# Head outputs copied once and stacked by on-chip transfers, and the low-part pass one unit later, in an adaLN block of attention and Mish feed-forward

## The chip, the cores and the metric

The kernel runs on one core of a Trainium2 chip. Its time is the device time of one execution in microseconds, the median of several. Matrix products run on TensorE (PE in the profile, its weight loads PEld), elementwise work on VectorE (DVE), ScalarE (ACT) and GpSimd (POOL); nearly all transfers are issued by SyncE (SP), one after the other, in the order of the program. An engine works through its own instructions in order; a semaphore wait at the head of a queue holds all that is behind it.

## The reference

One block with S = 2048 rows, D = 448, 16 heads of 28, a sliding window of 256 keys, a feed-forward width of 1792 and fp32 data:

```python
mod = (_silu(c) @ w_mod).reshape(c.shape[0], 6, 1, -1)
sa, ca, ga, sb, cb, gb = (mod[:, 0], mod[:, 1], mod[:, 2], mod[:, 3], mod[:, 4], mod[:, 5])
h = _layernorm(x, axis=-1) * (1 + ca) + sa
x = x + ga * _A_ref(h, A_wqkv, A_wo)     # windowed attention, softmax over (q-k >= 0) & (q-k < 256)
h = _layernorm(x, axis=-1) * (1 + cb) + sb
x = x + gb * _B_ref(h, B_w1, B_b1, B_w2) # dense, h * tanh(softplus(h)), dense
return x
```

## The kernel before

All products are made in fp32r with the operands split in two: a high part that ScalarE writes as fp32r and a low part, the difference. A product is then three passes (high x high, high x low, low x high).

**Groups, slots, units.** The 2048 rows are 4 groups of 512. In a group every head is a *slot* (64 in all, `NS`), and every slot has three *units* (192, `NU`) of 512 score columns: the blocks of keys that touch the window. The main loop (lines 1046 to 1107) runs over units `u`, with `s, k = divmod(u, 3)`: slot `s`, third `k`, group `g = s // 16`. What it issues in one step is the order of every engine's queue:

- `A(i, t)`: scores of slot `i`, 128 rows at a time, for the row maximum (TensorE into the bank `sA`, two buffers, then VectorE). It runs three slots ahead. `M2` turns the maxima of two slots into rows `mr`, and two small transfers put them into the extra rows of Q (`q<-mr`).
- `B(u)`: scores with keys on the partitions, masks added (bank `sB`, two buffers), then ScalarE's two exponentials from it: `P` in fp32 and `Ph` in fp32r, three buffers each.
- `SP(u-1)`: GpSimd's subtraction `Pl = P - Ph` (the last five units shared with VectorE).
- `PV`: products with V, high pass `PV(u-2, Ph)` at the end of a step, low pass `PV(u-3, Pl)` at the start of the next. V has 60 columns: 28 high, one of ones whose product is the softmax sum, and 28 low from column 32. So the bank `pv` of a head (two buffers) holds in rows 0 to 31 one part of its output and in rows 32 to 59 the other.
- `EV(i, part)`: ScalarE copies these two parts, one copy each, to the place of the head in `O4` and `OL4`, where four heads (a *quad*) stand one above the other at 32 partitions each. For the last three heads VectorE makes the second copy.
- For each quad `QA` (GpSimd, `O4 + OL4`), `T1` (VectorE, transposes in blocks of 32 and the reciprocal of the sums), `TM` (GpSimd, times the reciprocal), `T2` (VectorE, transposes back). After `T2` of the fourth quad of a group the group's attention is in `on_full`.
- `load_slot(s + 5)`: two transfers bring Q and K of a later slot from `scr` in HBM, where the projections are put. `need` first makes sure that the projection tiles of that head are stored: it flushes the stores that wait in `later` and, where a tile is missing, runs filler. The load waits on SyncE's queue for those stores to land.

**Filler.** Between these, `fill_main(g)` gives out the matmuls of other work as a generator: the rest of this group's projections (tiles 5, 2, 6), then, once `on_full` has the group before, its output projection (`gen_oT`, `gen_wo`), then the next group's transposed LayerNorm output (`gen_hT`) and its projections. Each piece tells its cost; each unit adds a credit `RATE[g]` (twice as much in the first units of a group, `FRONT`), and pieces are issued until the credit is spent. A step that waits for `on_full` costs one `RATE`. What is left at a group's end is issued in one go (`drain`). `fill_side` does the same for LayerNorm statistics and weights on the other engines, and `later` holds transfers that are issued one at a time.

**The end.** `TAIL` puts the first feed-forward matmuls between the last units; then the feed-forward stage (lines 1108 to 1181) follows.

In SBUF the pool `att` has the tiles `P`, `Ph` and `Pl` of 2 KB per partition and buffer. The transfers' scratch is left at its default size.

Of the kernel before, what the change touches and what calls it, by code (L numbers as in the profile page):

```python
# [8 lines left out]
F32 = mybir.dt.float32  # L9
F32R = mybir.dt.float32r  # L10
BF16 = mybir.dt.bfloat16
AF = mybir.ActivationFunctionType
ALU = mybir.AluOpType

S, D, F, H, DH, W = 2048, 448, 1792, 16, 28, 256
NG, GT = 4, 512
# [35 lines left out]
def adaln_block(ctx: ExitStack, tc: tile.TileContext, x, wqkv, wo, w1, b1, w2, c, w_mod, out):  # L52
    nc = tc.nc
    PE, ACT, DVE, POOL = nc.tensor, nc.scalar, nc.vector, nc.gpsimd
# [3 lines left out]
    def dma(o, i):  # L58
        nc.sync.dma_start(o, i)
# [31 lines left out]
    def bank(tag, bufs, name):  # L91
        return PS[0].tile([128, 512], F32, name=name, tag=tag, bufs=bufs)
# [163 lines left out]
    def tr_chunk(xs, ci, p):  # L256
        for t in range(4):
            PE.transpose(p[:, t * 128:(t + 1) * 128], xs[t][:, ci * 128:(ci + 1) * 128], ident)
# [5 lines left out]
    def hT_hi(p, ci, hh, si):  # L264
        ACT.activation(hh[:, ci], p, AF.Identity, scale=cols[:, si + 1, ci:ci + 1], bias=cols[:, si, ci:ci + 1])
# [6 lines left out]
    def new_T(key, pl):  # L272
        return (pl.tile([128, 4, GT], F32R, name=f"hh{key}", tag="hh"),
                pl.tile([128, 4, GT], F32R, name=f"hl{key}", tag="hl"))
# [20 lines left out]
    def gen_hT(g):  # L295
        drain(ln1[g])
        hh, hl = HT[g] = new_T(g, mid)
        for ci in range(4):
            p = bank("mm", 2, f"tr{g}{ci}")
            tr_chunk(XS[g], ci, p)  # L300
            pipe.add(2, lambda p=p, ci=ci: hT_hi(p, ci, hh, 0), lambda p=p, ci=ci: hT_lo(p, ci, hh, hl, 0))
            yield 1.9
        ht_done.add(g)
        if g + 1 < NG:
            loads = (lambda: x_load(g + 1),) if g > 1 else (lambda: (x_tile(g + 1), x_half(g + 1, 0)),
                                                            lambda: x_half(g + 1, 2))
            pipe.add(0, None, None, lambda: later.extend(loads))
# [5 lines left out]
    def drain(*gs):  # L313
        for g in gs:
            for _ in g:
                pipe.step()
# [17 lines left out]
    def flush():  # L334
        while later:
            later.pop(0)()
# [185 lines left out]
    att, att_s = pool("att")  # L522
# [1 line left out]
    Q3 = [Q2[i // 2][:, i % 2] for i in range(NQ)]  # L524
    k3_tile(att, NK - 1)

    O4, OL4, T4 = [att.tile([128, GT], F32, name=n) for n in ("o4", "ol4", "t4")]
    POOL.memset(OL4, 0.0)
    wo3 = [mid.tile([128, D], F32R, name=f"wo3_{i}", tag="wo", bufs=8) for i in range(4)]
    wol = [mid.tile([128, D], F32R, name=f"wol_{i}", tag="wo", bufs=8) for i in range(4)]  # L530
# [143 lines left out]
    NS = NG * H  # L674
    mx, Pt, Ph, Pl, pvb = {}, {}, {}, {}, {}
# [34 lines left out]
    def B(u):  # L710
        i, b = divmod(u, 3)
        g, h = divmod(i, H)
        q, k = Q3[i % NQ], K3[i % NK]
        bl = units(g, b)
        c0 = bl[0][3]
        p = bank("sB", 2, f"sB{u}")
        for n, (jj, t0, t1, c) in enumerate(by_width(bl)[::-1]):
            PE.matmul(p[:, c:c + 128 * (t1 - t0)], k[:, jj * 128:(jj + 1) * 128], q[:, t0 * 128:t1 * 128],  # L718
                      start=(n == 0), stop=False, skip_group_check=True)
        far = {c + 128 * (jj - t0) for jj, t0, t1, c in bl if t0 <= jj < t1}  # L720
        diag = {c + 128 * (jj - 2 - t0) for jj, t0, t1, c in bl if t0 <= jj - 2 < t1}
        masked = []
        for c in sorted(far | diag):
            if c in far:
                masked.append((256 if c + 128 in diag else 128, c, 0))
            elif c - 128 not in far:
                masked.append((128, c, 128))
        for n, c, m in sorted(masked):
            PE.matmul(p[:, c:c + n], identr, fdmask[:, m:m + n], start=False, stop=True, skip_group_check=True)  # L729
        P = Pt[u] = att.tile([128, 512], F32, name=f"P{u}", tag="P", bufs=3)  # L730
        Ph[u] = att.tile([128, 512], F32R, name=f"Ph{u}", tag="Ph", bufs=3)
        ACT.activation(P[:, c0:], p[:, c0:], AF.Exp, scale=SCALE)  # L732
        ACT.activation(Ph[u][:, c0:], p[:, c0:], AF.Exp, scale=SCALE)  # L733

    def SP(u):
        i, b = divmod(u, 3)
        c0 = units(i // H, b)[0][3]
        Pl[u] = att.tile([128, 512], F32R, name=f"Pl{u}", tag="Pl", bufs=3)
        for eng, a, b in ((POOL, c0, 512),) if u < NU - 5 else ((POOL, 0, 256), (DVE, 256, 512)):
            eng.tensor_tensor(Pl[u][:, a:b], Pt[u][:, a:b], Ph[u][:, a:b].bitcast(F32), op=ALU.subtract)  # L740

    def PV(u, P):
        i, b = divmod(u, 3)
        g, h = divmod(i, H)
        if P is Ph and b == 0:
            pvb[i] = bank("pv", 2, f"pv{i}")
        pv = pvb[i]
        for n, (jj, t0, t1, c) in enumerate(by_width(units(g, b))):
            j = 4 * g - 2 + jj
            PE.matmul(pv[0:60, t0 * 128:t1 * 128], V[j % NV][:, h, :], P[u][:, c:c + 128 * (t1 - t0)],  # L750
                      start=(P is Ph and b == 0 and n == 0), stop=False, skip_group_check=True)

    def EV(i, part):
        a = i % 4 * 32
        if part == 0:
            ACT.activation(O4[a:a + 32], pvb[i][0:32, :], AF.Copy)
        elif i < NS - 3:
            ACT.activation(OL4[a:a + DH], pvb[i][32:60, :], AF.Copy)
        else:
            DVE.tensor_copy(OL4[a:a + DH], pvb[i][32:60, :])  # L760

    def quad(qd):
        g, ci = divmod(qd, 4)
# [4 lines left out]
    def QA(qd):  # L768
        o, t = quad(qd)
        for eng, a, b in ((POOL, 0, GT),) if qd < NS // 4 - 1 else ((POOL, 0, 192), (DVE, 192, GT)):  # L770
            eng.tensor_tensor(o[:, a:b], O4[:, a:b], OL4[:, a:b], op=ALU.add)
# [3 lines left out]
    def T1(qd):  # L775
        o, t = quad(qd)
        DVE.transpose(T4, o)
        rcq[qd] = att.tile([128, 16, 1], F32, name=f"rc{qd}", tag="rc", bufs=1)
        DVE.reciprocal(rcq[qd], t[:, :, 28:29])
# [6 lines left out]
    def T2(qd):  # L786
        o, t = quad(qd)
        DVE.transpose(o, T4)
        if qd % 4 == 3:
            on_full.add(qd // 4)  # L790
# [204 lines left out]
        if not (told.get(g) == "bank" and pipe.held() or told.get(g) in taken):  # L995
            told[g] = next(side[g], None)

    RATE = {0: 0.64, 1: 1.02, 2: 1.02, 3: 0.65}
    FRONT = {0: 0, 1: 2, 2: 2, 3: 2}
    ln1 = {g: gen_ln1(g) for g in range(1, NG)}  # L1000
    fillers = {g: fill_main(g) for g in range(NG)}
# [2 lines left out]
    def step(g):  # L1004
        return next(fillers[g], 99.0) or RATE[g]

# [37 lines left out]
    NU = 3 * NS  # L1044
    credit = 0.0
    for u in range(NU + 9):
        s, k = divmod(u, 3)
        g = s // H
        if k == 0 and s % H == 0 and 0 < g < NG:
            drain(fillers[g - 1], side[g - 1])  # L1050
            flush()
        pipe.step()
        if 0 <= u - 3 < NU:
            PV(u - 3, Pl)
            if k == 2 and s % 4 != 1:
                EV(s - 1, 0)
        if k == 0 and 0 <= s - 2 < NS:
            if s % 4 == 2:
                EV(s - 2, 0)
            EV(s - 2, 1)  # L1060
        qd = (s - 5) // 4
        if k == 1 and s % 4 == 1 and 0 <= qd < NS // 4:
            QA(qd)
        if u < NU:
            B(u)
        if 0 <= u - 1 < NU:
            SP(u - 1)
        a = s + LEAD
        if a < NS:
            A(a, (0, 1, 3)[k])  # L1070
        if k == s % 2 and s < NS:
            load_slot(s + LEAD + 2)
        if k == 2 and s % 4 == 1 and 0 <= qd < NS // 4:
            T1(qd)
        qd = (s - 6) // 4
        if s % 4 == 2 and 0 <= qd < NS // 4:
            if k == 0:
                TM(qd)
            if k == (2 if u < NU else 0):
                T2(qd)  # L1080
        if g < NG:
            v = u - 48 * g
            if v in (0, 12):
                chunk["v"] = 4 if v == 0 and g or 0 < g < NG - 1 else 2
            if v == 0:
                credit = 0.0
            credit += RATE[g] * (2 if v < FRONT[g] else 1)
            while credit > 0.0:
                credit -= step(g)
        if k == 0 and (a - 1) % 2 == 1 and LEAD <= a - 1 < NS:  # L1090
            M2((a - 1) // 2)
        if g < NG:
            if v > 1 or g == 0:
                side_step(g, ("dve", "act")[a >= NS:] if k == 1 else ("act",) if k == 0 and s % 2 == 0 else ())
            if later and ((s + (k == 2)) % 2 == 0 or k == 1):
                later.pop(0)()
        if u == NU:
            drain(fillers[NG - 1], side[NG - 1])
            while pipe.items:
                pipe.step()  # L1100
            flush()
        if u - NU in TAIL:
            TAIL[u - NU]()
        if k == 1 and a < NS:
            A(a, 2)
        if 0 <= u - 2 < NU:
            PV(u - 2, Ph)
# [53 lines left out]
    for n in range(NN + 1):  # L1161
        g, f = divmod(n, NF)
# [44 lines left out]
```

## Time and profile before

| | |
|---|---|
| median of 3 runs | 729.16 us (728.52 to 729.28) |
| the profiled execution | 729.9 us |
| its span, first to last instruction | 728.1 us |
| mean granted clock of TensorE | 0.983 |
| bytes moved by transfers | 83.74 MB, 115 GB/s on the mean |

The main loop's first unit begins about 47 us after the start of the span, and the last attention output is copied at about 430 us. In rows of the profile a name such as `Pl<-P,Ph` is the tile written and those read; L740 is a line of the kernel; "x192 | 234.1, 1226 | 95.1" are the count, the busy time in us, the mean duration in ns, and the idle time of the engine before them in us. Rows of waits give the total in us, how often, and the longest. SPq stands for SyncE's queue, whose rows are issues of transfers and not their duration; `q<-mr` or `k<-scr` names a transfer as destination and source. A wait that depends on several semaphores is put down to the one that came last.

### The profile page before, as it was taken

The numbers are of one execution on the slowest core, as the hardware profiler recorded it, in microseconds if no ns is written. First come the engines' busy times: TensorE is split into PE (matmuls) and PEld (weight loads), VectorE is DVE, ScalarE is ACT, GpSimd is POOL, SyncE is SP. The second block draws the span as 40 slices with busy tenths as digits, with TensorE's granted clock in tenths as the row PEclk, the third lists the DMA queues.
The fourth block names the chain that finished last, engine by engine and source line by source line (L and its number), as shares of the span: only waits on it lengthen the run. The fifth ranks groups of instructions, "written<-read, shape, count | busy, mean of one in ns | idle before, by whom it ended". The sixth has DMA issues, their size and how long they took to land.

```text
span 728.1 us, 11809 instructions
## 1 busy us (share of the span) xinstructions
PE 688.9 (95%) x3873; PEld 582.3 (80%) x3873; DVE 399.7 (55%) x992; ACT 429.5 (59%) x784; POOL 348.7 (48%) x363
## 2 busy tenths in 40 slices
PE   8998989989989989999999889999999999999996
PEld 7776767779778778788778668888888888888885
DVE  5678657668847668765788876242424133323112
ACT  4559878788857688877898984334233223322221
POOL 6536778687846687856888947332010000000002
PEclk9999999989999989999999999999999999999998
DMA  7854763364373354275484145500200020001001
GB/s 221 256 197 165 213 187 127 107 204 147 83 251 120 102 184 159 72 232 152 147 274 154 53 137 181 151 14 1 101 1 1 0 102 1 0 1 51 0 1 50
DMA packets 48330, 83.74 MB, mean 115 GB/s; under 512 B 6287, under 2 KB 26429, under 8 KB 48269
## 3 DMA queue, kind: packets, MB, share of 16 engines
q1 hardware_dynamic: 47804, 82.98, 36.4%
q8 instruction: 31, 0.51, 0.3%
q14 instruction: 31, 0.25, 0.1%
q10 hardware_dynamic: 464, 0.00, 0.0%
HBM read 53.34 MB, written 29.36 MB: 114 GB/s over the span
## 4 chain that ended last, share of the span: by engine, by line
PE 65%; issue 12%; DVE 7%; ACT 6%; DMA 6%; POOL 2%; SPq 1%; POOLq 0%; DVEq 0%; ACTq 0%
PE z L932 14%; PE pv L750 8%; PE qk L323 7%; PE wo L323 5%; PE acc L1126 4%; PE acc L1127 4%; PE acc L1125 4%; PE sA L688 4%; PE sB L718 4%; PE qk_v L323 3%; PE sB L729 3%; DMA scr<-st 2%; DMA k<-scr 2%; ACT Ph L733 2%; DVE junk L690 2%
## 5 line engine op out<-in xcount | busy, mean ns | idle before, releaser
L740 POOL TENSOR_TENSOR Pl<-P,Ph 128x512 fp32r<-128x512 f32 (+2 forms) x192 | 234.1, 1226 | 95.1 <-ACT Ph L733 60.2
L690 DVE CUSTOM_DVE_ANT_0 junk<-sA,mask 128x384 bf16<-128x384 f32 (+2 forms) x256 | 134.9, 527 | 87.9 <-PE sA L688 75.2
L938 ACT ACTIVATE t<-z,b1c 128x512 f32<-128x512 f32 x56 | 38.5, 687 | 192.0 <-PE z L932 188.9
L940 DVE TENSOR_TENSOR al<-t,ah 128x512 fp32r<-128x512 f32 x56 | 40.3, 719 | 189.6 <-ACT ah L939 189.6
L732 ACT ACTIVATE P<-sB 128x512 f32<-128x512 f32 (+2 forms) x192 | 110.1, 573 | 36.9 <-PE sB L729 32.4
L733 ACT ACTIVATE Ph<-sB 128x512 fp32r<-128x512 f32 (+2 forms) x192 | 109.6, 571 | 0.0
L688 PE MATMUL sA<-k,q 84*128 84x384 f32 (+2 forms) x256 | 100.4, 400 | 9.5 <-DMA k<-scr 5.1
L932 PE MATMUL z<-hhf,w 128*128 128x512 f32 x224 | 89.3, 399 | 0.0
L932 PE MATMUL z<-hlf,w 128*128 128x512 f32 x224 | 88.4, 395 | 0.0
L750 PE MATMUL pv<-Pl,v 128*60 128x256 f32 (+2 forms) x352 | 76.6, 292 | 10.6 <-POOL Pl L740 8.4
L718 PE MATMUL sB<-q,k 86*128 86x256 f32 (+1 forms) x352 | 77.4, 294 | 5.4 <-ACT Ph L733 2.5
L1126 PE MATMUL acc<-w2l,ah 128*128 128x448 f32 x224 | 81.6, 364 | 0.4 <-POOL w2l L902 0.4
L1125 PE MATMUL acc<-w2h,ah 128*128 128x448 f32 x224 | 81.8, 365 | 0.0
L1127 PE MATMUL acc<-w2h,al 128*128 128x448 f32 x224 | 81.7, 365 | 0.0
L750 PE MATMUL pv<-Ph,v 128*60 128x256 f32 (+2 forms) x352 | 79.5, 300 | 0.0
L718 PEld LDWEIGHTS sB<-q,k 86*128 86x128 f32 x352 | 62.0, 194 | 10.6 <-ACT Ph L733 5.3
L932 PE MATMUL z<-hhf,w1l 128*128 128x512 f32 x168 | 66.3, 395 | 0.0
L750 PEld LDWEIGHTS pv<-Pl,v 128*60 128x60 f32 x352 | 44.8, 135 | 24.2 <-POOL Pl L740 15.9
L688 PEld LDWEIGHTS sA<-k,q 84*128 84x128 f32 x256 | 49.4, 196 | 16.4 <-DVE mx L690 7.0
L729 PE MATMUL sB<-fdmask,identr 128*128 128x128 bf16 (+1 forms) x320 | 61.2, 257 | 0.0
L750 PEld LDWEIGHTS pv<-Ph,v 128*60 128x60 f32 x352 | 46.6, 136 | 13.0 <-issue 1.1
L1134 POOL TENSOR_TENSOR yo<-yo,x 128x448 f32<-128x448 f32 (+1 forms) x4 | 4.2, 1064 | 108.1 <-DVE yo L1131 108.1
(157 smaller groups left out, 1325.6 us busy)
## 6 DMA issues: line engine op xcount, KB each, us to landing
scr<-st SPq DMA_DIRECT2D x24, 512.0 KB
k<-scr SPq DMA_DIRECT2D x48, 252.0 KB
q<-scr SPq DMA_DIRECT2D x64, 168.0 KB
scr<-st SPq DMA_DIRECT2D x32, 256.0 KB
x<-x1d SPq DMA_DIRECT2D x10, 448.0 KB
xin<-in_A_x_dram SPq DMA_DIRECT2D x8, 448.0 KB
xr<-in_A_x_dram SPq DMA_DIRECT2D x16, 224.0 KB
x1d<-xr SPq DMA_DIRECT2D x16, 224.0 KB
```

The costliest lines, as they stand in the source:

```text
L323: PE.matmul(p, b, a, start=(n == 0), stop=(n == len(ps) - 1))
L688: PE.matmul(p[:, c0:384], q[0:84, t * 128:(t + 1) * 128], k[0:84, t * 128 + c0:t * 128 + 384], start=True, stop=True)
L690: DVE.tensor_tensor_reduce(out=junk[:, c0:384], in0=p[:, c0:384], in1=mask[:, c0:384], scale=1.0, scalar=-3.0e38, op0=ALU.add, op1=ALU.max ...
L718: PE.matmul(p[:, c:c + 128 * (t1 - t0)], k[:, jj * 128:(jj + 1) * 128], q[:, t0 * 128:t1 * 128], start=(n == 0), stop=False, skip_group_ch ...
L732: ACT.activation(P[:, c0:], p[:, c0:], AF.Exp, scale=SCALE)
L733: ACT.activation(Ph[u][:, c0:], p[:, c0:], AF.Exp, scale=SCALE)
L740: eng.tensor_tensor(Pl[u][:, a:b], Pt[u][:, a:b], Ph[u][:, a:b].bitcast(F32), op=ALU.subtract)
L750: PE.matmul(pv[0:60, t0 * 128:t1 * 128], V[j % NV][:, h, :], P[u][:, c:c + 128 * (t1 - t0)], start=(P is Ph and b == 0 and n == 0), stop=F ...
L932: PE.matmul(zb[n], ps[m][1], ps[m][0], start=(m == 0), stop=(m == 10))
L1125: PE.matmul(p, ah[n][:, ts], w2h[f], start=(f == 0), stop=False)
L1126: PE.matmul(p, ah[n][:, ts], w2l[f], start=False, stop=False)
L1127: PE.matmul(p, al[n][:, ts], w2h[f], start=False, stop=(f == NF - 1))
```

## The change

1. `EV(i)` is now one ScalarE copy of all 60 rows of the bank to half of a new tile `O2` (heads alternate between partitions 0 and 64). It comes at `k == 0` two slots after the head's own. `EM(i)`, one unit later and at the end of its step, puts the two parts in their places in `O4` and `OL4` with two transfers on SyncE's queue. The last four heads are copied as the last three were before.
2. The low pass is `PV(u-4, Pl)` in place of `PV(u-3, Pl)`, and `P`, `Ph` and `Pl` have four buffers.
3. `QA`, `T1`, `TM` and `T2` of a quad are issued at slots `4 qd + 6` (thirds 0, 1, 2) and `4 qd + 7` (third 1); before, `QA` and `T1` came at slot `4 qd + 5` (thirds 1 and 2), `TM` and `T2` at `4 qd + 6` (thirds 0 and 2). The last quad's four come together.
4. Credits: `RATE` 0.62, 0.97, 0.97, 0.65 for 0.64, 1.02, 1.02, 0.65, and 1.5 for 1.9 as the cost of one step of `gen_hT`.
5. `dynamic_dma_scratch_size=1024`: the scratch is 1 KB per partition.

```diff
-            yield 1.9
+            yield 1.5
...
-    O4, OL4, T4 = [att.tile([128, GT], F32, name=n) for n in ("o4", "ol4", "t4")]
+    O4, OL4, T4, O2 = [att.tile([128, GT], F32, name=n) for n in ("o4", "ol4", "t4", "o2")]
...
-        P = Pt[u] = att.tile([128, 512], F32, name=f"P{u}", tag="P", bufs=3)
-        Ph[u] = att.tile([128, 512], F32R, name=f"Ph{u}", tag="Ph", bufs=3)
+        P = Pt[u] = att.tile([128, 512], F32, name=f"P{u}", tag="P", bufs=4)
+        Ph[u] = att.tile([128, 512], F32R, name=f"Ph{u}", tag="Ph", bufs=4)
...
-        Pl[u] = att.tile([128, 512], F32R, name=f"Pl{u}", tag="Pl", bufs=3)
+        Pl[u] = att.tile([128, 512], F32R, name=f"Pl{u}", tag="Pl", bufs=4)
...
-    def EV(i, part):
-        a = i % 4 * 32
-        if part == 0:
+    def EV(i):
+        a, b = i % 4 * 32, i % 2 * 64
+        if i < NS - 4:
+            ACT.activation(O2[b:b + 60], pvb[i][0:60, :], AF.Copy)
+        else:
             ACT.activation(O4[a:a + 32], pvb[i][0:32, :], AF.Copy)
-        elif i < NS - 3:
-            ACT.activation(OL4[a:a + DH], pvb[i][32:60, :], AF.Copy)
-        else:
             DVE.tensor_copy(OL4[a:a + DH], pvb[i][32:60, :])
+
+    def EM(i):
+        a, b = i % 4 * 32, i % 2 * 64
+        if i < NS - 4:
+            dma(O4[a:a + 32], O2[b:b + 32])
+            dma(OL4[a:a + DH], O2[b + 32:b + 60])
...
-    RATE = {0: 0.64, 1: 1.02, 2: 1.02, 3: 0.65}
+    RATE = {0: 0.62, 1: 0.97, 2: 0.97, 3: 0.65}
...
-        if 0 <= u - 3 < NU:
-            PV(u - 3, Pl)
-            if k == 2 and s % 4 != 1:
-                EV(s - 1, 0)
-        if k == 0 and 0 <= s - 2 < NS:
-            if s % 4 == 2:
-                EV(s - 2, 0)
-            EV(s - 2, 1)
-        qd = (s - 5) // 4
-        if k == 1 and s % 4 == 1 and 0 <= qd < NS // 4:
+        qd = (s - 6) // 4
+        if s % 4 == 2 and 0 <= qd < NS // 4 - 1 and k == 0:
             QA(qd)
+        if 0 <= u - 4 < NU:
+            PV(u - 4, Pl)
+            if k == 0:
+                EV(s - 2)
...
-        if k == 2 and s % 4 == 1 and 0 <= qd < NS // 4:
-            T1(qd)
-        qd = (s - 6) // 4
-        if s % 4 == 2 and 0 <= qd < NS // 4:
-            if k == 0:
+        if 0 <= qd < NS // 4 - 1:
+            if s % 4 == 2 and k == 1:
+                T1(qd)
+            if s % 4 == 2 and k == 2:
                 TM(qd)
-            if k == (2 if u < NU else 0):
+            if s % 4 == 3 and k == 1:
                 T2(qd)
+        if k == 0 and s - 2 == NS - 1:
+            for f in (QA, T1, TM, T2):
+                f(NS // 4 - 1)
...
+        if k == 1 and 0 <= s - 2:
+            EM(s - 2)
...
-    nc = _bacc.Bacc("TRN2", target_bir_lowering=False, num_devices=1)
+    nc = _bacc.Bacc("TRN2", target_bir_lowering=False, num_devices=1, dynamic_dma_scratch_size=1024)
```

## The prediction

> **What bounds the kernel now.** I read the page first, then busy time by stretch, then the waits of TensorE, then the time order of single queues where the waits are longest. In the page, TensorE is busy nearly throughout and no other engine is near its limit; but that is a mean over an attention stage (about 47 to 426 us) and a feed-forward stage that the change leaves alone.
>
> ```profile
> PE 688.9 (95%) x3873; PEld 582.3 (80%) x3873; DVE 399.7 (55%) x992; ACT 429.5 (59%) x784; POOL 348.7 (48%) x363
> L758 ACT ACTIVATE ol<-pv 28x512 f32<-28x512 f32 x61 | 35.9, 588 | 1.3
> ```
>
> By stretch (start:end, length, then busy us of PE, PEld, DVE, ACT, POOL, granted clock, DMA share, GB/s):
>
> ```profile
> 142.00:156.00 14.00, 10.14 (x58) 8.24 (x57) 10.40 (x31) 10.93 (x22) 10.71 (x11) 0.76 0.68 212
> 250.00:264.00 14.00, 10.83 (x63) 8.58 (x61) 10.64 (x31) 11.23 (x22) 10.73 (x12) 0.76 0.72 230
> 264.00:352.00 88.00, 86.04 (x567) 74.45 (x568) 61.30 (x179) 71.50 (x132) 63.91 (x54) 1.00 0.48 149
> 398.00:426.00 28.00, 22.60 (x160) 17.25 (x159) 24.17 (x52) 27.48 (x52) 25.14 (x27) 1.00 0.18 58
> ...
> 430.00:446.00 16.00, 15.59 (x73) 13.35 (x72) 12.91 (x14) 10.77 (x20) 11.25 (x9) 1.00 0.82 256
> ```
>
> Where there is filler work (264:352), TensorE is full: 86.04 of 88 us. There, time saved on ScalarE is worth nothing. It can be worth something in two kinds of place: the last attention stretch, where ScalarE is busy 27.48 of 28 us, and the short waits before it. Two stretches stand out, 142:156 and 250:264, at the start of groups 1 and 2: TensorE idles 3 to 4 us there and its clock falls to 0.76. Here are TensorE's waits between 50 and 400 us, its matmuls' own and those before its weight loads (total us, times, longest):
>
> ```profile
> PE pv L750 <- POOL Pl L740: 6.0, 9, 2.1
> ...
> PE sB L718 <- ACT Ph L733: 2.5, 8, 0.5
> PE sB L718 <- ACT ol L758: 1.7, 1, 1.7
> ...
> PEld pv L750 <- POOL Pl L740: 11.9, 19, 2.4
> PEld sB L718 <- ACT Ph L733: 5.3, 11, 0.8
> ```
>
> The change bears on the rows for Pl and Ph: 8.5 us by the matmuls' own records, 17.2 by the loads'. With the last stretch below, this bounds any gain.
>
> **The change part by part.**
>
> *One copy for two.* 60 heads lose the copy at L758. The remaining one moves 60 rows instead of 32; the 28-row copy (588 ns) and the 32-row copy (583, below) show that rows don't price it. So ScalarE loses 61 x 0.588 = 35.9 us (head 60's second copy goes to VectorE). That counts only where ScalarE is last, as in the last stretch:
>
> ```profile
> L756 ACT ACTIVATE o<-pv 32x512 f32<-32x512 f32 x6 | 3.5, 583 | 0.2
> L758 ACT ACTIVATE ol<-pv 28x512 f32<-28x512 f32 x4 | 2.4, 588 | 0.1
> ```
>
> Four copies fall in it, 2.4 us. The waits of the weight loads there, on Pl, show how much could go in all:
>
> ```profile
> PEld pv L750 <- POOL Pl L740: 4.1, 6, 1.6
> PEld pv L750 <- DVE Pl L740: 2.1, 2, 1.1
> ```
>
> Bounds: 0 (GpSimd, 25.14 of 28, takes over as the limit) to -6.2. I take **-2.4**: an engine that is 98% busy gives back what is taken off it, and little more while GpSimd is close behind.
>
> *Low-part pass a unit later, fourth buffers.* TensorE meets Pl(u) one unit later, about 2 us more for GpSimd to finish (379 us of attention over 192 units). Apart from the two group starts, treated next, waits of 6.0 - 2.1 - 1.3 on Pl and 2.5 on the score bank remain in the matmuls' own records, 5.1 us; by weight loads 11.9 - 2.4 - 1.7 + 5.3 = 13.1, but loads also stand idle while a matmul still runs. The rows taken off:
>
> ```profile
> PE pv L750 <- POOL Pl L740: 2.1, 1, 2.1
> ...
> PE pv L750 <- POOL Pl L740: 1.3, 1, 1.3
> ...
> PEld pv L750 <- POOL Pl L740: 2.4, 1, 2.4
> ...
> PEld pv L750 <- POOL Pl L740: 1.7, 1, 1.7
> ```
>
> Bounds 0 to -13.1; I take **-5.1**, time in which the array itself certainly stood.
>
> *120 transfers on SyncE's queue, and what waits behind them.* Each head's pair (EM) is 64 and 56 KB, and SyncE issues in order. EM(i) stands behind `load_slot` in its step, and QA on GpSimd, two units after the fourth head's EM, now waits for a landing; behind QA stand all later Pl subtractions, and VectorE's T1, behind which stand the row maxima that free the sA banks. Usually this is covered: an on-chip row transfer lands 1.77 us after its issue by the chain of waits, and two units are about 4 us.
>
> ```profile
> 53.88 1.77 DMA q<-mr
> ```
>
> It isn't at a group's start. The unit that issues EM(15) first stores a projection tile and loads a head's K, which must wait for that store. SyncE's queue there, before:
>
> ```profile
> 138.63 1.36 SPq L59 DMA_DIRECT2D q<-mr  x2
> 140.09 0.90 SPq L59 DMA_DIRECT2D scr<-st  x2
> 141.08 0.68 SPq L59 DMA_DIRECT2D q<-scr  x1
> 143.96 0.32 SPq L59 DMA_DIRECT2D k<-scr  x1
> 144.40 0.89 SPq L59 DMA_DIRECT2D scr<-st  x2
> ```
>
> and GpSimd's:
>
> ```profile
> 137.07 1.29 POOL L771 TENSOR_TENSOR on<-o,ol 128x512 f32<-128x512 f32 x1
> ...
> 142.37 1.28 POOL L740 TENSOR_TENSOR Pl<-P,Ph 128x512 fp32r<-128x512 f32 x1 [0.66 <-PE sA L688]
> ...
> 145.69 0.24 POOL L233 TENSOR_SCALAR rsa<-mva 128x4 f32<-128x4 f32 x1 [1.14 <-DVE mva L220]
> ...
> 147.60 2.49 POOL L740 TENSOR_TENSOR Pl<-P,Ph 128x512 fp32r<-128x512 f32 x2
> ```
>
> QA ran at 137.07. Afterwards EM(15) can be issued at 144.4 and, 0.4 us later, 144.8; landed at 144.8 + 1.77 = 146.6; QA to 147.9; the Pl that stood at 142.37 to 149.2; the variance work (145.69 to 147.60, 1.9) to 151.1; the Pl that ended at 147.60 + 1.25 = 148.85 then ends at 152.4, 3.5 us later. TensorE may take it one unit later. A unit here lasts 2.0 to 2.2 us, between these rows of the chain:
>
> ```profile
> 148.92 0.68 PE pv L750 x2
> ...
> 150.91 0.85 PE pv L750 x4
> ...
> 153.07 0.85 PE pv L750 x4
> ```
>
> So TensorE loses 3.5 - 2.1 = 1.4 at group 1, and the same at group 2. At group 3 a K load holds TensorE anyway until 353.50 + 4.59 = 358.1, after QA (353.9 + 0.4 + 1.8 + 1.3 = 357.4):
>
> ```profile
> 349.57 3.88 DMA scr<-st
> ...
> 353.50 4.59 DMA k<-scr
> ```
>
> Nothing for that one while the K load is last; if it weren't, 3.5. Bounds for the three: -3.4 (landing in time, the 2.1 and 1.3 gone) to +10.5. I take **+2.8**.
>
> The Trainium skill, DMA: Bandwidth & Descriptors, Anatomy of one DMA, gives a fixed cost of about 2.0 us plus bytes over 436 GB/s, some 2.15 us for 64 KB (an estimate by that page). The row's 1.77 us is for 4 KB and agrees on the scale; by the page the two group starts would cost 0.4 us more each, and its advice against two transfers to disjoint partition halves (Rules for kernel authors) speaks against stacking heads this way.
>
> *Row transfers.* Around 100 us, weight loads fill SyncE's queue, and a unit waited 1.7 us in the row above that names ol. It waited for the row transfer q<-mr as well, whose second issue, at about 104.4, lands 1.77 later, at 106.2. EM(8) adds two issues ahead:
>
> ```profile
> 100.69 2.79 SPq L59 DMA_DIRECT2D wop<-in_A_wo_dram  x4
> 103.58 1.48 SPq L59 DMA_DIRECT2D q<-mr  x2
> 105.16 0.40 SPq L59 DMA_DIRECT2D q<-scr  x1
> ```
>
> Two issues of 0.40: **+0.8**, bounds 0 (room before 103.58) to +1.6 (EM(9) too).
>
> *At nothing.* The lower credits (0.62, 0.97, 1.5) and T2 two units later shift when filler runs, not how much; hidden by `need`, which pulls tiles forward, and by `drain`; -1 to +2 if it moves out of, or into, units with room. The last Pl pass moves behind six z matmuls, hidden by the filler and feed-forward matmuls that keep TensorE busy 15.59 of 16 us at 430:446; uncovered, six z matmuls of 0.4 (next row), 2.4.
>
> ```profile
> L932 PE MATMUL z<-hhf,w 128*128 128x512 f32 x224 | 89.3, 399 | 0.0
> ```
>
> The smaller scratch: all traffic but instruction fetch is hardware_dynamic, so no queue can lose by it.
>
> ```profile
> q1 hardware_dynamic: 47804, 82.98, 36.4%
> ```
>
> **Sum:** -2.4 - 5.1 + 2.8 + 0.8 = -3.9. The profiled execution took 729.9 us (span 728.1 and 1.8 around it), so 726.0; the median of the runs lies 0.7 lower, 729.16, so **725.3**.
>
> **The rivals.**
> *Bigger gain.* The pair lands before QA needs it even at group starts, and with those waits go the clock drops. For it: the 2.1 and 1.3 us on Pl there, and a clock of 0.76 over 14 us, which is 14 x 0.24 = 3.4 us lost at each. Against: the queue rows above. -2.4 - 5.1 - 3.4 and one clock drop of the two, -3.4: 715; with half of the last two terms, 718.
> By the Trainium skill, TensorE: Matmul & The Clock Gate, The HAM clock gate, the clock halves after an idle window of about 3.4 us; the trace agrees so far as the clock is 0.76 in the two stretches with such waits and 1.00 at 264:352.
>
> *Slower: QA's wait stops GpSimd in every quad.* In any quad the fourth head's EM comes behind the row transfer and the loads of its step; 1.4 for the row transfer, 0.4 + 0.4 for the loads, 0.8 for the pair and 1.8 to its landing are 4.8 us (rows above) against 4 us or less for two units. 0.8 us at 15 quads is 12 us of GpSimd standing still, 18 if two units are 3.6; it decides once GpSimd has under a unit in hand, as at 398:426 (25.14 of 28) and in the group starts. With half of it on TensorE, +9, and the two group starts at 3.5 in place of 1.4, +4.2: -3.9 + 13.2 = +9.3, 738; with a third of the 18 alone, +6: +2.1, 731. Against it: TensorE full for most of groups 1 to 3.
>
> *No change.* ScalarE's and GpSimd's waits only hand over to VectorE (24.17 of 28 in the last stretch): -2.4 and half of -5.1 gone, so -2.6 + 3.6 = +1.0, 730.
>
> **How the numbers follow.** Forecast 0.42; bigger gain 0.13; slower 0.32; no change 0.13. This kernel's measurement tells 0.2%, 1.5 us, from nothing. The forecast's own range, 721 to 728.5, spills a little into no change: faster 0.51, same 0.15, slower 0.34. The range for 8 in 10 reaches to most of both sides: 718 to 736.
>
> **What would show it.** Right: ScalarE near 394 us busy; waits of pv on Pl between 50 and 400 us under 3 us; TensorE's stall at the start of groups 1 and 2 as long as before or longer, with QA waiting on a transfer o4 or ol4; 398:426 shorter by 2 to 3 us. Wrong: QA waiting on landings in most quads, or GpSimd's subtractions later than now at full filler; or those group starts gone, with the clock back at 1.00.

## The result, and the profile after

The changed kernel takes 768.2 us (median of 4 runs, 766.8 to 769.1) where the kernel before takes 728.9 in the same series (728.5 to 729.3): a ratio of 1.0538 [1.0519, 1.0557], 39 us slower. Forecast were 725.3 us and a range of 718 to 736. The profiled execution took 768.7 us, its span is 766.9 and its mean clock 0.962. One slow run of 1324.9 us, of the version below with two sets of O4 and OL4, is left out of that version's median.

The page of the changed kernel, busy time and the costliest lines:

```profile
PE 701.2 (91%) x3873; PEld 594.2 (77%) x3873; DVE 397.6 (52%) x993; ACT 392.1 (51%) x723; POOL 347.9 (45%) x363
...
L756 ACT ACTIVATE o<-pv 60x512 f32<-60x512 f32 x60 | 35.3, 589 | 41.7 <-PE pv L750 39.2
```

ScalarE came out as worked out: 392.1 us (forecast near 394), and one copy of 60 rows takes 589 ns, as one of 28 did. So ScalarE's work did shrink; what grew is idle time. The attention stage as a whole, by stretch, before and then after:

```profile
47.00:426.00 379.00, 351.16 (x2251) 291.29 (x2250) 271.73 (x768) 309.75 (x592) 281.46 (x252) 0.97 0.49 154
```

```profile
47.00:464.00 417.00, 361.93 (x2243) 300.60 (x2242) 265.52 (x762) 269.83 (x526) 278.95 (x250) 0.93 0.52 158
```

The stage is 38 us longer, nearly all of the loss; about as many matmuls are spread over it, and the granted clock fell from 0.97 to 0.93. 379 x 0.03 = 11 us and 417 x 0.07 = 29: up to 18 of the 38 us are clock, not waiting. GpSimd's subtractions and QAs, grouped by line and shape (before, then after), say where the idle time went:

```profile
L740 POOL TENSOR_TENSOR Pl<-P,Ph 128x512 fp32r<-128x512 f32 x155 | 202.7, 1314 | 82.3 <-ACT Ph L733 50.1 <-PE pv L750 9.7 <-POOL Pl L740 7.4
L771 POOL TENSOR_TENSOR on<-o,ol 128x512 f32<-128x512 f32 x15 | 20.1, 1338 | 0.9 <-DVE hlo L631 0.7 <-PE sA L688 0.2
```

```profile
L740 POOL TENSOR_TENSOR Pl<-P,Ph 128x512 fp32r<-128x512 f32 x155 | 202.0, 1316 | 56.2 <-ACT Ph L733 40.6 <-POOL Pl L740 4.9 <-PE pv L750 4.7
...
L776 POOL TENSOR_TENSOR on<-o,ol 128x512 f32<-128x512 f32 x15 | 19.1, 1273 | 70.6 <-DMA ol<-o 35.9 <-PE sA L688 18.5 <-DMA q<-scr 6.1
```

Before, GpSimd stood 0.9 us ahead of its 15 QAs; now 70.6, on average 4.7 each. The releasers TensorE and `q<-scr` in that row are the inference's: QA reads only `O4` and `OL4`, which from here on only the pairs of transfers fill, and by the landings in the trace each of the 15 starts 0.1 to 0.6 us after its quad's last transfer has landed. Who waits in turn, over the whole span (before, then after):

```profile
PEld pv L750 <- POOL Pl L740: 15.9, 25, 2.4
PE pv L750 <- POOL Pl L740: 8.4, 12, 2.1
```

```profile
DVE t L782 <- POOL on L776: 38.0, 14, 4.6
PEld pv L750 <- POOL Pl L740: 36.3, 18, 4.5
PE pv L750 <- POOL Pl L740: 30.5, 14, 4.3
PE sB L718 <- DMA q<-mr: 8.5, 6, 3.7
```

One quad from end to end, the one that the prediction worked out: EM(15) at the start of group 1. The changed kernel's time order on SyncE's queue, GpSimd, VectorE and TensorE (start, duration, what; in brackets the idle time before), and the stretch that follows:

```profile
148.02 1.37 SPq L59 DMA_DIRECT2D q<-mr  x2
149.48 0.91 SPq L59 DMA_DIRECT2D scr<-st  x2
150.48 0.68 SPq L59 DMA_DIRECT2D q<-scr  x1
153.27 0.32 SPq L59 DMA_DIRECT2D k<-scr  x1
153.69 0.56 SPq L59 DMA_DIRECT2D o<-o  x1
154.30 0.80 SPq L59 DMA_DIRECT2D ol<-o  x1
...
158.50 0.56 SPq L59 DMA_DIRECT2D o<-o  x1
```

```profile
149.83 1.29 POOL L740 TENSOR_TENSOR Pl<-P,Ph 128x512 fp32r<-128x512 f32 x1 [0.30 <-POOL Pl L740]
157.21 1.26 POOL L776 TENSOR_TENSOR on<-o,ol 128x512 f32<-128x512 f32 x1 [6.09 <-DMA q<-scr]
158.43 1.26 POOL L740 TENSOR_TENSOR Pl<-P,Ph 128x512 fp32r<-128x512 f32 x1
```

```profile
158.50 0.71 DVE L782 STREAM_TRANSPOSE t<-on 128x512 f32<-128x512 f32 x1 [3.42 <-POOL on L776]
```

```profile
159.74 0.68 PE L750 MATMUL pv<-Pl,v 128*60 128x128 f32 x2 [3.93 <-POOL Pl L740]
```

```profile
160.00:176.00 16.00, 13.73 (x72) 10.96 (x72) 11.11 (x29) 12.57 (x24) 15.77 (x17) 0.71 0.61 171
```

Read it downwards. The pair of the fourth head stands behind two row transfers, two stores and two loads; the K load waits for the stores until 153.27. The pair is issued from 153.69 to 155.10, and 2.1 us later QA starts. GpSimd has stood for 6.09 us with subtractions queued behind QA; VectorE stood 3.42, TensorE 3.93. Then the clock is 0.71 for the next 16 us, which costs up to 16 x 0.29 = 4.6 us of TensorE's time beside the stall itself; the kernel before lost up to 3.4 us to the clock at this place (0.76 over 14 us), so only a part of that is new. And the next head's pair, at 158.50, had to wait for QA to have read `O4` (157.21 + 1.26 = 158.47), with everything on SyncE's queue behind it.

An ordinary quad in group 2, with nothing stored in between:

```profile
291.70 1.37 SPq L59 DMA_DIRECT2D q<-mr  x2
293.17 0.41 SPq L59 DMA_DIRECT2D q<-scr  x1
293.63 0.65 SPq L59 DMA_DIRECT2D k<-scr  x1
294.37 0.56 SPq L59 DMA_DIRECT2D o<-o  x1
294.98 0.81 SPq L59 DMA_DIRECT2D ol<-o  x1
```

```profile
297.88 1.28 POOL L776 TENSOR_TENSOR on<-o,ol 128x512 f32<-128x512 f32 x1 [1.93 <-PE sA L688]
```

From the first row transfer to QA are 6.2 us: 1.4 + 1.2 + 1.4 of issues with the gaps between them, and 2.1 from the last issue's end. This is one of the milder quads.

### The profile page after: what moved, and what is told of

Read it like the earlier page. It is cut to its first block, busy times and chain, and to the rows that moved or that the text cites. A ratio compares the mean times of both kernels' runs of the same rounds, so it can differ in the third digit from the quotient of the medians.

```text
span 766.9 us, 11988 instructions
## 1 busy us (share of the span) xinstructions
PE 701.2 (91%) x3873; PEld 594.2 (77%) x3873; DVE 397.6 (52%) x993; ACT 392.1 (51%) x723; POOL 347.9 (45%) x363
## 4 chain that ended last, share of the span: by engine, by line
PE 65%; issue 13%; DMA 8%; DVE 6%; POOL 3%; ACT 3%; SPq 1%; POOLq 0%; ACTq 0%; DVEq 0%
PE z L937 14%; PE pv L750 8%; PE qk L323 7%; PE wo L323 5%; PE sB L718 4%; PE acc L1132 4%; PE acc L1130 4%; PE acc L1131 4%; DMA ol<-o 4%; PE sA L688 4%; PE sB L729 3%; PE qk_v L323 2%; DVE junk L690 2%; POOL Pl L740 2%; PE warm L436 1%
## 5 line engine op out<-in xcount | busy, mean ns | idle before, releaser
L688 PE MATMUL sA<-k,q 84*128 84x384 f32 (+2 forms) x256 | 104.1, 416 | 7.5 <-DVE mx L690 6.2
L750 PE MATMUL pv<-Pl,v 128*60 128x256 f32 (+2 forms) x352 | 79.0, 300 | 30.6 <-POOL Pl L740 30.5
L718 PE MATMUL sB<-q,k 86*128 86x256 f32 (+1 forms) x352 | 80.5, 304 | 14.2 <-DMA q<-mr 8.5
L750 PE MATMUL pv<-Ph,v 128*60 128x256 f32 (+2 forms) x352 | 82.1, 309 | 0.0
L718 PEld LDWEIGHTS sB<-q,k 86*128 86x128 f32 x352 | 65.4, 205 | 19.7 <-issue 8.8
L750 PEld LDWEIGHTS pv<-Pl,v 128*60 128x60 f32 x352 | 47.3, 141 | 42.3 <-POOL Pl L740 36.3
L688 PEld LDWEIGHTS sA<-k,q 84*128 84x128 f32 x256 | 51.9, 207 | 15.6 <-DVE mx L690 10.9
L729 PE MATMUL sB<-fdmask,identr 128*128 128x128 bf16 (+1 forms) x320 | 63.8, 267 | 0.0
L750 PEld LDWEIGHTS pv<-Ph,v 128*60 128x60 f32 x352 | 48.8, 142 | 13.8 <-issue 2.0
L756 ACT ACTIVATE o<-pv 60x512 f32<-60x512 f32 x60 | 35.3, 589 | 41.7 <-PE pv L750 39.2
```

The lines of the kernel that those rows point to most:

```text
L688: PE.matmul(p[:, c0:384], q[0:84, t * 128:(t + 1) * 128], k[0:84, t * 128 + c0:t * 128 + 384], start=True, stop=True)
```

## The experiments

Ratios are to the kernel before in the same series (its median was 728.6, 728.2, 728.1 and 726.9 in the four). Theory T says that QA's wait for the landings, and what is queued behind QA on GpSimd, is the loss; theory Q that the 120 transfers crowd out the row transfers `q<-mr`, wherever QA stands; theory L that the later low pass is at fault.

**The later low pass alone, and with the credits.** The kernel before with four buffers for `P`, `Ph` and `Pl`, the scratch of 1 KB and

```diff
-        if 0 <= u - 3 < NU:
-            PV(u - 3, Pl)
-            if k == 2 and s % 4 != 1:
-                EV(s - 1, 0)
-        if k == 0 and 0 <= s - 2 < NS:
-            if s % 4 == 2:
+        if 0 <= u - 4 < NU:
+            PV(u - 4, Pl)
+            if k == 0:
                 EV(s - 2, 0)
-            EV(s - 2, 1)
+                EV(s - 2, 1)
```

> The kernel before with the low pass one unit later, fourth buffers and the small scratch; both copies by ScalarE straight into the quad tiles, no transfers, credits as before. Theory T (GpSimd's QA stands until transfers land, and the subtractions behind it hold TensorE): no transfers, so 720 to 728. Theory Q (the transfers crowd SyncE's queue and the max rows come late): no transfers either, 720 to 728. Theory L (the lag or the order of the low pass itself costs): 745 or more.

Measured: 724.3 us, ratio 0.9951 [0.9928, 0.9973]. TensorE's waits in it:

```profile
PE sB L718 <- ACT Ph L733: 8.0, 13, 1.3
```

The waits on `Pl` fell from 8.4 to 2.6 us, but the scores now wait for ScalarE, 8.0 in place of 2.5, where two copies in a row stand ahead of the next exponentials. The second run adds the changed credits to it.

> e1_lag_only with the changed kernel's credits (0.62, 0.97, 1.5). If the credits only move filler, 722 to 728, as e1. If they are part of the loss, 730 or more.

Measured: 722.0 us, 0.9926 [0.9905, 0.9946]. L falls: the later pass is worth 4 to 6 us. The lower credits do no harm. Of the versions that leave nothing out this is the fastest: 6 us less than the kernel before and 46 less than the changed one.

**The later pass taken out of the changed kernel.** `PV(u - 3, Pl)` and three buffers again, all else as changed.

> The changed kernel with the low pass back at its old place and three buffers: stacking by transfers alone. Theory T (QA's wait for landings holds the subtractions behind it): TensorE meets the late subtractions a unit sooner, 770 to 790. If the lag itself did harm beside transfers: 766 or less.

Measured: 799.1 us, 1.0992 [1.0965, 1.1018], above the range expected.

```profile
PE pv L750 <- POOL Pl L740: 59.9, 21, 6.2
```

Without the extra unit TensorE meets QA's delay a unit earlier, and the waits double. Within the changed kernel the later pass is worth 799.1 - 768.2 = 31 us, against 4 in the kernel before: it is cover for T.

**QA's wait taken away, the transfers kept.**

```diff
+    O5, OL5 = [att.tile([128, GT], F32, name=n) for n in ("o5", "ol5")]
...
-            eng.tensor_tensor(o[:, a:b], O4[:, a:b], OL4[:, a:b], op=ALU.add)
+            eng.tensor_tensor(o[:, a:b], O5[:, a:b], OL5[:, a:b], op=ALU.add)
```

> The changed kernel, all 120 transfers issued, but QA adds two constant tiles that no transfer writes, so GpSimd waits for no landing (the attention output is left out of the result). T: most of the 39 us goes, 728 to 738. Q: the queue is as crowded as it was, 755 or more. L: 760 or more.

Measured: 732.5 us, 1.0063 [1.0039, 1.0087]. The wait, with what it brings in its train, is worth 768.2 - 732.5 = 36 us of the 39. But the kernel is then still not where the gains would put it:

```profile
PE sB L721 <- DMA q<-mr: 15.4, 7, 5.9
```

**The transfers taken away as well.** The same kernel with `EM` empty.

> The changed kernel without its 120 transfers, and with QA reading two constant tiles as in the run with QA's wait taken away (732.5 us): attention's output does not enter the result here, all other work is as in the changed kernel. It splits that run's time into the gain of copying once and the price of the transfers by themselves. Theory (transfers alone cost about 10 us beside the wait, through late row maxima q<-mr, the rest of the change gains): 715 to 723, waits of the scores on q<-mr back under 5 us, a saving against 732.5 of 10 to 17. Rival (the transfers by themselves are hidden, and the late rows come from the order of the queue, which the credits changed): 729 to 733, with the waits on q<-mr still above 8 us.

Measured: 716.5 us, 0.9853 [0.9817, 0.9890].

```profile
PE sB L721 <- DMA q<-mr: 6.1, 6, 3.0
```

That wait is a little above the 5 us expected, and the kernel before has 0.7 us of it: some of the rows' lateness is there without any transfer. The transfers by themselves cost 16 us, with no one waiting for them but the rows and loads behind them. The time between the first score products of units 0, 48, 96, 144 and 190, from the traces, places both prices:

| us per group | 0 | 1 | 2 | 3 |
|---|---|---|---|---|
| before | 80.4 | 107.8 | 103.6 | 82.5 |
| later pass and credits, no transfers (722.0) | 80.0 | 104.0 | 99.9 | 84.1 |
| all but transfers and wait (716.5) | 79.7 | 100.3 | 100.5 | 81.8 |
| transfers, no wait (732.5) | 86.6 | 101.2 | 101.5 | 85.6 |
| changed | 90.8 | 115.8 | 111.4 | 96.9 |

The transfers' own cost lies in group 0 (6.9 us of 12.7), where weight loads fill the queue; the wait's cost lies in all four (4.2, 14.6, 9.9, 11.3).

**The pair ahead of the rows and loads.** `EM(s - 2)` right behind `EV(s - 2)` in the order of the program.

> The changed kernel with the pair of transfers issued right behind its copy, ahead of the max rows and the loads of the next unit on SyncE's queue. T: the pair lands 3 to 7 us earlier where it stood behind a load, QA's waits fall by more than half, 735 to 750. Q: the max rows now stand behind the pair, 768 or more. L: 768.

Measured: 740.4 us, 1.0168 [1.0130, 1.0206].

```profile
PE sB L718 <- DMA q<-mr: 20.4, 11, 6.3
```

GpSimd's idle time ahead of its 15 QAs falls to under 3 us in all, and 28 us come back; but the row maxima now stand behind a pair that waits for its copy, and TensorE waits 20.4 us for them. On one in-order queue one of the two is late.

**Two sets of O4 and OL4, QA's chain three units later.**

```diff
+    O4s, OL4s = [[att.tile([128, GT], F32, name=f"{n}{j}") for j in range(2)] for n in ("o4", "ol4")]
...
-        qd = (s - 6) // 4
-        if s % 4 == 2 and 0 <= qd < NS // 4 - 1 and k == 0:
+        qd, w = divmod(u - 18 - 3, 12)
+        if w == 0 and 0 <= qd < NS // 4 - 1:
             QA(qd)
```

> The changed kernel with two sets of quad tiles (O4, OL4) in turn and QA, T1, TM, T2 three units later, so that five units lie between the last pair's issue and QA. T: waits of 2 to 6 us mostly covered by 6 us more, 728 to 742. Q: same queue, 758 or more. L: 760 or more.

Measured: 740.4 us, 1.0174 [1.0135, 1.0214]. 28 us come back, by giving the landing time instead of place in the queue; a wait of 15.2 us for `q<-mr` remains.

**The pairs on ScalarE's queue.** `ACT.dma_start` in place of `dma` in `EM`, which comes at the end of step `k == 0`.

> The changed kernel with the 120 transfers issued from ScalarE's queue, behind the exponentials of the same unit: neither behind SyncE's loads nor ahead of its max rows. T and Q together: both kinds of wait go, waits of TensorE on q<-mr under 4 us, 722 to 735, less what issuing costs ScalarE. If landing itself is slow or the traffic costs: 745 or more.

Measured: 729.9 us, 1.0021 [0.9999, 1.0043]: no change against the kernel before, 38 us less than the changed one. GpSimd waits 0.9 us in all for landings ahead of QA. The pair is also issued a unit earlier than in the changed kernel, which the run doesn't separate from the queue. The Trainium skill, DMA: Bandwidth & Descriptors, Rules for kernel authors, says that spreading transfers over issuing engines adds no bandwidth and saves only issue time. Here the same bytes are moved and 38 us are saved, and 28 us came back on SyncE's own queue by an earlier place in line (740.4): the place counts, not only the time of the issues. Of TensorE's waits one stays, and SyncE's queue shows the place of its longest piece:

```profile
PE sB L718 <- DMA q<-mr: 12.3, 6, 6.7
```

```profile
103.66 5.71 SPq L59 DMA_DIRECT2D wop<-in_A_wo_dram  x12
109.47 0.90 SPq L59 DMA_DIRECT2D scr<-st  x2
110.47 1.39 SPq L59 DMA_DIRECT2D q<-mr  x2
```

Twelve weight loads stand ahead of rows that VectorE had ready at 103.87; in the kernel before four stood ahead and eight behind. The next run asks whether this order, which the credits set, is what remains of Q.

> The pairs are issued by ScalarE's queue as in the run before of this kind (729.9 us), but the filler's credits are those of the kernel before (0.64, 1.02, 1.02, 0.65 and 1.9). What is asked: why TensorE still waited 12.3 us for the row maxima q<-mr there, 6.8 of it at once at 104 to 113 us. In that trace VectorE had the rows mr ready at 103.87, and SyncE issued them at 110.47, because twelve weight loads wop and two stores stood ahead of them; in the kernel before only four of these loads stand ahead of the rows and eight come behind. Theory of the order (the lower credits move the loads ahead of the rows, and the pairs make that order late): with the old credits only four wop loads stand ahead of those rows, the wait for q<-mr at that place is under 2 us, and the time is 721 to 726. Rival (the pairs fill the DMA rings and semaphores, whatever the order): the waits for q<-mr stay above 8 us in all and the time is 728 to 731.

Measured: 731.0 us, 1.0046 [1.0023, 1.0069], and 15.6 us of waiting for `q<-mr`. The theory of the order misses: four loads stood ahead, and the rows, which VectorE had ready at 101.33, were late all the same.

```profile
101.51 4.47 SPq L59 DMA_DIRECT2D wop<-in_A_wo_dram  x4
106.08 1.49 SPq L59 DMA_DIRECT2D q<-mr  x2
```

```profile
SPq L59 <- DMA o<-o: 12.7, 7, 3.7
```

These four loads took 4.47 us; the next four in the same queue took 1.6. The second view, SyncE's own waits, says for what: 12.7 us for landings of pairs that another engine issued and that no load reads. In the trace all transfers signal eight semaphores in turn, and an issue waits until the transfer that used its semaphore before has landed: the load issued at 103.58 waited for a transfer of a pair, issued by ScalarE at 100.07, to land at 103.57. So the pairs hold up SyncE even from another queue. With the pairs on SyncE's own queue (732.5 us) it stands only 0.7 us for landings of pairs, so there such waits are hardly a part of the 16 us; how these divide between the issues and their place in line was not separated.

> The changed kernel with the credits of the kernel before, nothing else. If the lower credits only decide the order of some loads and rows (theory of the order), they are worth here what they are worth with the pairs on ScalarE's queue, at most: 760 to 768, with the wait of GpSimd's QA for landings unchanged at 60 to 75 us of idle time. If the credits are no part of the loss at all: 766 to 770. If they were set to make up for the transfers, so that the old ones are worse here: above 771.

Measured: 770.4 us, 1.0568 [1.0529, 1.0606], beside 1.0538 [1.0519, 1.0557] for the changed kernel, and GpSimd stands 71.8 us ahead of its QAs (70.6 there): the credits are no part of the loss.

**Two attempts at a better version.** Both move a copy of the version with two copies per head: one unit later, and to VectorE.

```diff
-            if k == 0:
-                EV(s - 2, 0)
-                EV(s - 2, 1)
+        if k < 2 and 0 <= s - 2 < NS:
+            EV(s - 2, k)
```

> e1_lag_only with ScalarE's two copies of a head one unit apart. In e1 they stand together ahead of a unit's exponentials, and TensorE's waits for a score bank rose from 2.5 to 8.0 us. If these waits are from the pair of copies: half of them go, 719 to 723. If not: 724 to 727.

Measured: 728.2 us, 1.0012 [0.9990, 1.0034], a miss. GpSimd's waits in it:

```profile
POOL on L771 <- ACT ol L758: 15.7, 10, 2.1
```

The scores' wait for `Ph` shrank to 5.0 us, but the last copy of a quad now comes in the same step as QA, just ahead of it in the order of the program, and GpSimd stands for it as it does for the landings.

```diff
-        elif i < NS - 3:
+        elif i < NS - 3 and i % 2 == 0:
             ACT.activation(OL4[a:a + DH], pvb[i][32:60, :], AF.Copy)
```

> The best kernel so far (the low pass a unit later, four buffers, the changed credits, two copies per head, no transfers: 722.0) with the second copy of every odd head on VectorE in place of ScalarE. 30 copies of about 0.6 us leave ScalarE, so the two copies no longer stand ahead of the next exponentials in every slot. If the scores' wait for ScalarE's Ph (about 8 us in the kernels of this kind) is what is left: 717 to 721. If VectorE, whose row maxima free the score banks sA, pays as much as ScalarE gains: 722 to 726.

Measured: 740.4 us, 1.0177 [1.0150, 1.0204], above both ranges.

```profile
PE sA L688 <- DVE mx L690: 20.1, 28, 2.8
DVE ol L760 <- ACT o L756: 14.7, 18, 1.9
```

VectorE's copy waits 14.7 us for ScalarE's copies, and the row maxima behind it come late: TensorE waits 20.1 us for them, against 4.6 in the version that this one starts from. It is the same fault again, on VectorE.

## Why the prediction was wrong, step by step

**The step that failed** is "Usually this is covered: an on-chip row transfer lands 1.77 us after its issue by the chain of waits, and two units are about 4 us." Two units were sized right: in the ordinary quad above GpSimd stood ready for QA at 297.88 - 1.93 = 295.95, 4.25 us after the first row transfer. What was set against them was wrong in three sizes. The pair's issue costs 0.56 + 0.81 with a gap, 1.4 us, where 0.4 to 0.8 were put: 0.4 was the issue of a load, a row at hand but of another kind. From the start of the second issue to QA pass 2.9 us in both quads shown (154.30 to 157.21, 294.98 to 297.88), where 1.77 was put; that row counts from the start of an issue too, but of a transfer of 4 KB. And the pair waits in line for what it doesn't need: rows whose maxima VectorE hasn't made, K loads that wait for stores. So QA was late in nearly every quad, by 4.7 us on average, which the prediction itself had named as a sign of being wrong; and the term of +2.8 for two group starts measured 732.5 to 768.2, +36.

The landing is no constant either. In another quad QA started 4.5 us after the last issue's end, where the two quads above have 2.1:

```profile
204.18 0.81 SPq L59 DMA_DIRECT2D ol<-o  x1
...
209.50 1.26 POOL L776 TENSOR_TENSOR on<-o,ol 128x512 f32<-128x512 f32 x1 [6.10 <-DMA ol<-o]
```

The Trainium skill, DMA: Bandwidth & Descriptors, Anatomy of one DMA, gives 2.0 us and 0.13 for 56 KB (an estimate by that page, whose fit is for transfers issued by GpSimd). The first two quads agree with it if it is counted from the issue's end; the third doesn't.

**The rival that named this** ("QA's wait stops GpSimd in every quad") had the mechanism, the place and the count of 15 right, and the share that reaches TensorE came out too: half was put, and 36 of 70.6 us is half. That is luck in part, because TensorE's own waits on `Pl` grew by 22 us (8.4 to 30.5), and the lower clock, up to 18 us in the stage, was not in the rival's sum. Its shortage per quad, 0.8 to 1.2 us, was about a fifth of the real one, so it gave 738 where 768 came. Its 4.8 us chain had no wait of SyncE in it. It also missed the loop: the pair of the next head must not overwrite what QA has yet to read, so a late QA holds SyncE's queue in turn.

```profile
SPq L59 <- POOL on L776: 26.9, 13, 4.7
```

And it let the stall cost only itself. The 3.93 us stall above was followed by 16 us at 0.71. The Trainium skill, TensorE: Matmul & The Clock Gate, The HAM clock gate, names an idle window of about 3.4 us for that. The 3.93 us fit it, but here a shorter stall was enough, and the measurement decides. In the kernel before, TensorE stood 1.61 us, was busy 1.80 of the 3.41 us up to 253.39, and had half the clock for the 6.7 us behind:

```profile
252.98 0.44 PE L688 MATMUL sA<-k,q 84*128 84x384 f32 x1 [1.61 <-DVE mx L690]
```

```profile
249.98:253.39 3.41, 1.80 (x15) 1.42 (x13) 3.34 (x10) 3.37 (x7) 2.18 (x2) 1.00 0.69 201
253.40:260.10 6.70, 5.44 (x27) 4.37 (x25) 3.72 (x14) 4.40 (x9) 5.73 (x8) 0.50 0.88 308
```

**Row transfers, +0.8 with bounds 0 to +1.6:** the place, the weight loads around 100 us, was right, the size was not. Group 0 alone lost 6.9 us, the four groups 12.7 by the table, the whole run 16. The term took two issues at 0.40; it left out that six pairs (heads 6 to 11) are issued between 90 and 125 us and that each takes 1.4 us.

**Later pass and fourth buffers, -5.1:** measured -4 alone and -6 with the credits. The total is right. Of its two parts the waits on `Pl` went as described (8.4 to 2.6 us over the span), but those on the score bank, which were to go too, rose from 2.5 to 8.0, so the total is right by luck in part.

**One copy for two, -2.4 in the last stretch:** the sum was saved, but elsewhere. From unit 176 to unit 190 the kernel before takes 22.7 us, and so does the kernel without transfers and wait. The reason given, that an engine 98% busy gives back what is taken off it, didn't hold; GpSimd, busy 25.14 of 28 us there, is the likely limit behind it, which no run tried. Beside the version with the later pass alone the gain of copying once, and of a QA chain that stands for nothing, is 722.0 to 716.5, about 5 us, in groups 1 and 3. What the two traces show of it is the scores' wait for ScalarE: 8.8 us with two copies per head, 2.5 with one.

**At nothing:** the credits measured as that. From unit 190's first product to the end of the span the kernel before takes 306.8 us and the changed one 305.1, so the last low pass behind the z matmuls cost nothing. The smaller scratch was never run alone.

Put together, as ratios of 728.9 us: later pass and credits -5.4, one copy -5.3, transfers +15, the wait +35. The forecast had -5.1, -2.4, +0.8 and +2.8: both gains were there, and both costs were 12 to 20 times what they were put at.

## What to carry to other kernels

An operation that waits for a transfer on an in-order engine prices everything queued behind it: work out the whole line to the landing, the producer's queue included, for an ordinary round and not only for the worst, and add the waits of the transfers ahead of it, not only their issues. When work is moved from an engine that isn't the limit to a queue that others need in time, the saved busy time is no gain and the place in line is the cost; look for another queue or give the reader more rounds. Where stalls are followed by a lower granted clock, put a price on that too: here it was up to 18 of 38 us, nearly as much as the standing itself.

## What the runs showed of the hardware that was not expected

The two issues of a pair don't cost the same: 64 KB from 32 partitions take 0.56 us, 56 KB from 28 partitions 0.80, fewer bytes taking longer. The longer one is always the second; two row transfers of one shape in a row take 0.65 and 0.63 (medians), so the place alone hardly explains it, but no run separates shape and place. On ScalarE's queue the first costs the same 0.54 us, while ScalarE goes on computing (time order of the run with the pairs there):

```profile
87.60 0.54 ACTq L764 DMA_DIRECT2D o<-o  x1
87.88 0.48 ACT L733 ACTIVATE Ph<-sB 128x384 fp32r<-128x384 f32 x1
```

And transfers of different engines are tied to each other by the semaphores that they share: 12.7 us of SyncE's time went to landings of ScalarE's pairs.
